# Weights on 128 partitions and a TensorE loop over all 32 tiles, in a decode attention kernel

## The chip, the cores and the metric

The kernel runs on one core of a Trainium2 chip. The metric is device time in microseconds (us) of one execution. Names used below: PE is TensorE (matmuls), DVE VectorE, ACT ScalarE, POOL GpSimd, SP SyncE, whose queue issues all DMA loads here. The page is the profiler's summary of one execution, and the span is the length of that execution in the profile.

## The reference

One decode step for a batch of 4. Four query rows attend to a cache of 8192 keys and values in 8 KV heads, and the result is gated by a small MLP branch. The part that costs time is the cache: 4 x 8 = 32 (batch, head) pairs, each with 4 MB of K and 4 MB of V.

```python
xn = layernorm(A_x)                               # 4 x 448
q  = xn @ wq                                      # wq 448 x 4096 -> 16 heads of 256
p  = softmax(q . k_cache * 256**-0.5)             # per (batch, kv head): 8192 keys, 2 query heads
s  = (p . v_cache) @ wo                           # wo 4096 x 448
xn2 = layernorm(xn)
g  = silu(xn + gelu(xn2 @ w3) @ w4)               # w3 448 x 1792, w4 1792 x 448 (w1, w2 drop out at S = 1)
out = A_x + s * g
```

## The kernel before

A "tile" is one (batch, KV head) pair. For tile h, PE transposes K in 16 groups (T), DVE and ACT copy the transposes out of PSUM, PE makes the scores (S), and softmax follows. PE multiplies with V one tile later (PV), in the last six slots of tile h + 1. K and V have two buffers each. SP issues the loads in this order (cut):

```python
sp.dma_start(wq_sb..., A_wq.rearrange("(p j) n -> p (j n)", j=4))   # 112 partitions, 32 KB each
sp.dma_start(w3_sb..., B_w3.rearrange("(p j) n -> p (j n)", j=4))   # 112 partitions, 14 KB each
sp.dma_start(w4_sb..., B_w4.rearrange("(p k) n -> p (k n)", k=14))  # 128 partitions, 12.25 KB each
load_k(0); load_k(1); <load wo>; load_v(0)
for h in range(2, NH):
    load_k(h)          # waits until tile h-2 is transposed
    load_v(h - 1)      # waits until PV of tile h-3 is done
load_v(NH - 1)         # in four pieces
```

448 = 4 x 112, so `wq` and `w3` lie on 112 partitions. On PE the first two tiles were straight code, because tile 0 has no tile before it, and a loop did the other 30:

```python
body(0, prev=False)
body(1, first=True)
with nc.Fori(0, (NH - 2) // 2, engines=[PE], ...):
    body(2); body(3)
<scores, softmax and PV of the last tile, output projection>
```

All other engines run straight code for all 32 tiles.

## Time and profile before

677.12 us was the median of the first three runs. The table holds the quantities that matter; the fences show where they are read.

| Quantity | Before |
|---|---|
| data moved, span of the profiled run | 279 MB, 675.8 us |
| DMA rate in most slices | 431 to 434 GB/s |
| PE busy | 80% |
| DMA rate in the first 25 us | 210 to 308 GB/s |
| instruction packets of PE (queue 8) | 14 |

From the page of the kernel before: the span, PE and the DMA rate in 40 equal slices, and the DMA queues.

```profile
span 675.8 us, 27268 instructions
...
PE   0675687898788789888787988887888888878987
...
GB/s 237 367 402 426 431 430 427 394 433 434 433 434 431 431 433 433 431 429 431 433 430 434 433 434 433 431 431 433 433 427 431 431 433 433 433 434 433 433 412 47
...
q1 hardware_dynamic: 14176, 279.00, 97.6%
q8 instruction: 14, 0.23, 0.1%
q14 instruction: 9, 0.07, 0.0%
```

The flat 431 to 434 of most slices is taken as the limit: 279 MB at 433 GB/s alone take 644 us. The exceptions are the first three slices, slice 8 and the end. `q8` and `q14` are instruction fetches.

The same kernel in windows. Columns: window, its length, busy time and number of instructions of each engine, the granted PE clock, the DMA share and GB/s.

```profile
0.00:5.00 5.00, 0.00 (x0) 0.00 (x0) 2.34 (x10) 1.49 (x2) 1.53 (x10) 1.00 0.81 210
5.00:10.00 5.00, 1.09 (x8) 0.97 (x8) 3.57 (x14) 1.49 (x2) 0.00 (x0) 1.00 0.84 216
10.00:15.00 5.00, 0.00 (x0) 0.00 (x0) 0.00 (x0) 0.00 (x0) 0.00 (x0) 1.00 1.14 308
15.00:20.00 5.00, 2.08 (x78) 2.11 (x79) 0.00 (x0) 0.00 (x0) 0.00 (x0) 1.00 0.86 212
20.00:25.00 5.00, 2.27 (x70) 2.21 (x68) 0.48 (x4) 0.00 (x0) 0.31 (x2) 1.00 0.98 305
25.00:30.00 5.00, 3.11 (x48) 2.81 (x47) 1.25 (x6) 0.25 (x1) 0.00 (x0) 1.00 1.07 456
...
120.00:125.00 5.00, 2.32 (x71) 2.20 (x68) 1.38 (x2) 0.00 (x0) 0.00 (x0) 0.74 0.78 331
```

Until 25 us the DMA engines are busy (share 0.81 to 1.14) and yet move 210 to 308 GB/s, half to 0.7 of what they move later (the first window also holds 2.1 us in which no weight packet has started). So they have work; their packets are slow. In the window at 120 us the share falls: there they had no work.

Why they had none is in the timelines of PE and of the SP queue, before. "[2.49 <-issue]" is idle time ahead of an instruction that waited for nothing the profile shows. In these lines `kn` is a K tile, `vb` a V tile, and `pst`, `psc` and `psv` are the PSUM results of T, S and PV.

```profile
102.17 0.62 PE L463 MATMUL psv<-pT,vb 128*128 128x32 bf16 x17 [2.49 <-issue]
109.49 0.33 PE L436 MATMUL psc<-qc,kT 128*128 128x2 bf16 x7 [1.15 <-issue]
116.84 0.39 PE L463 MATMUL psv<-pT,vb 128*128 128x32 bf16 x9 [2.33 <-issue]
123.75 0.48 PE L424 MATMUL pst<-ident_b,kn 128*128 128x128 bf16 x3 [2.68 <-issue]
```

```profile
102.82 0.33 SPq L174 DMA_DIRECT2D vb<-in_A_v_cache_dram  x1
124.26 0.33 SPq L161 DMA_DIRECT2D kn<-in_A_k_cache_dram  x1
```

PE stops inside groups of identical matmuls. In the trace's packet records a 16 KB packet of queue 8 belongs to each stop (99.8, 106.9, 114.5, 121.2 us): it starts with the stop, in the second case 1.4 us before it, and PE goes on 1.3 to 1.5 us after each of these packets has ended. This is the loop's first round, and its code is only now fetched. After one at 125.1 us there is no more such packet until the tail (669.7). So the loop, two tiles with 1,556 matmuls and weight loads (389 of each per tile, by the counts on the page), is fetched once. Because of the stops the K load at 124.26 us was issued late.

### The profile page before, as it was taken

Reading aid. Unit: us, or ns where it says so; the run is one execution under the profiler, and the core shown is the slowest. Engines: PE = TensorE matmul, PEld = TensorE weight load, DVE = VectorE, ACT = ScalarE, POOL = GpSimd, SP = SyncE. Lnnn points to the kernel's source line nnn. Section 1 sums busy time; section 2 is a strip of 40 time slices with the busy share of each in tenths; the row PEclk is TensorE's granted clock in tenths of the full one; section 3 lists DMA queues with packets and bytes.
Section 4 is the critical chain, followed back from the end, with each engine's and each line's share of the span. In section 5 each row is a group of like instructions: output and inputs, shape, how many; then the busy total and the mean of one; then the engine's idle time right before and its main releaser. Section 6 shows DMA issues by size and latency. Waiting matters only on the chain. (4 is left out here: it accounts for less than half of the span.)

```text
span 675.8 us, 27268 instructions
## 1 busy us (share of the span) xinstructions
PE 540.1 (80%) x12686; PEld 526.7 (78%) x12686; DVE 241.1 (36%) x550; ACT 250.1 (37%) x358; POOL 7.4 (1%) x42
## 2 busy tenths in 40 slices
PE   0675687898788789888787988887888888878987
PEld 0575687898788789888787988877888888878985
DVE  3143133343333334333333433433333433333432
ACT  1043143354333344343233443433344333334440
POOL 0000000000000000000000000000000000000000
PEclk9978688798878998788789987888997877889889
DMA  9999999999999999999999999999999999999991
GB/s 237 367 402 426 431 430 427 394 433 434 433 434 431 431 433 433 431 429 431 433 430 434 433 434 433 431 431 433 433 427 431 431 433 433 433 434 433 433 412 47
DMA packets 14199, 279.29 MB, mean 413 GB/s; under 512 B 1145, under 2 KB 5249, under 8 KB 5249
## 3 DMA queue, kind: packets, MB, share of 16 engines
q1 hardware_dynamic: 14176, 279.00, 97.6%
q8 instruction: 14, 0.23, 0.1%
q14 instruction: 9, 0.07, 0.0%
HBM read 278.99 MB, written 0.00 MB: 413 GB/s over the span
## 5 line engine op out<-in xcount | busy, mean ns | idle before, releaser
L424 PE MATMUL pst<-ident_b,kn 128*128 128x128 bf16 x4096 | 363.9, 241 | 87.7 <-PEq L385 81.2
L221 ACT ACTIVATE kT<-pst 128x1024 bf16<-128x1024 bf16 x224 | 227.1, 1024 | 363.3 <-PE pst L424 363.3
L424 PEld LDWEIGHTS pst<-ident_b,kn 128*128 128x128 bf16 x4096 | 279.8, 108 | 94.4 <-issue 93.1
L219 DVE COPY kT<-pst 128x1024 bf16<-128x1024 bf16 x288 | 199.1, 692 | 388.3 <-PE pst L424 388.3
L436 PE MATMUL psc<-qc,kT 128*128 128x2 bf16 x4096 | 181.6, 165 | 1.9 <-issue 1.9
L436 PEld LDWEIGHTS psc<-qc,kT 128*128 128x128 bf16 x4096 | 169.6, 101 | 3.0 <-issue 3.0
L463 PE MATMUL psv<-pT,vb 128*128 128x32 bf16 x3968 | 128.6, 177 | 20.7 <-PEq L385 12.5
L463 PEld LDWEIGHTS psv<-pT,vb 128*128 128x128 bf16 x3968 | 113.4, 96 | 18.5 <-issue 18.5
L241 ACT ACTIVATE pT<-psc,negb 128x64 bf16<-128x64 f32 x64 | 20.2, 331 | 19.0 <-DVE negb L338 19.0
L212 POOL COPY qc<-qT 128x4 bf16<-128x4 bf16 x32 | 5.9, 187 | 620.4 <-PE psc L436 600.5
L241 ACT ACTIVATION_READ_ACCUMULATOR pT<-psc,negb 128x1 f32 x64 | 12.6, 196 | 0.0
L450 PE MATMUL psm<-diag,ones_f 2*128 2x2 f32 x64 | 12.1, 256 | 0.0
L455 PE MATMUL psm<-rowsum,ones_f 128*128 128x2 f32 x64 | 11.8, 254 | 0.0
L399 PE MATMUL pst<-xnT,vb 112*128 112x4 bf16 x128 | 3.6, 166 | 8.4 <-PEq L385 8.4
L450 PEld LDWEIGHTS psm<-diag,ones_f 2*128 2x128 f32 x64 | 9.4, 182 | 1.0 <-issue 0.4
L399 PEld LDWEIGHTS pst<-xnT,vb 112*128 112x128 bf16 x128 | 3.5, 104 | 8.4 <-issue 8.4
L455 PEld LDWEIGHTS psm<-rowsum,ones_f 128*128 128x128 f32 x64 | 9.8, 192 | 0.4 <-issue 0.4
L350 DVE TENSOR_TENSOR OT<-psv,rz 128x2 bf16<-128x2 f32 x63 | 7.4, 162 | 7.4 <-PE psc L518 3.1
L446 PE MATMUL psm<-ident_f,rmax 128*2 128x128 f32 x32 | 9.4, 294 | 0.6 <-PEq L385 0.6
L326 DVE TENSOR_REDUCE rmax<-psc 128x2 f32<-128x128 f32 x32 | 9.0, 281 | 0.4 <-PE psc L436 0.4
L331 DVE TENSOR_REDUCE gmax<-psm 2x1 f32<-2x128 f32 x32 | 8.6, 269 | 0.6 <-PE psm L446 0.6
L392 PE MATMUL pst<-ident_b,xn_b 4*112 4x4 bf16 x8 | 1.1, 236 | 8.5 <-DVE xn_b L279 5.9
(59 smaller groups left out, 68.0 us busy)
## 6 DMA issues: line engine op xcount, KB each, us to landing
kn<-in_A_k_cache_dram SPq DMA_DIRECT2D x32, 4096.0 KB, 23.1
vb<-in_A_v_cache_dram SPq DMA_DIRECT2D x31, 4096.0 KB, 32.1
vb<-in_A_v_cache_dram SPq DMA_DIRECT2D x4, 1024.0 KB, 17.7
vb<-in_A_wq_dram SPq DMA_DIRECT2D x1, 3584.0 KB, 16.6
wo_sb<-in_A_wo_dram SPq DMA_DIRECT2D x1, 3584.0 KB, 54.3
vb<-in_B_w_dram SPq DMA_DIRECT2D x2, 1568.0 KB, 24.6
x_sb<-in_A_x_dram SPq DMA_DIRECT2D x1, 3.5 KB
out_dram<-out_b SPq DMA_DIRECT2D x1, 3.5 KB
```

The source lines that it names most:

```text
L219: engine.tensor_copy(dst, src).then_inc(S["v_ev"], 1)
L221: engine.activation(dst, src, ACT.Copy).then_inc(S["a_ev"], 1)
L241: ins = act.activation(pv_p[:, :, hh], sc[:, :, hh], ACT.Exp, bias=negb[:, s, hh:hh + 1], scale=SCALE, accum_out=rowsum[:, s, hh:hh + 1])
L326: v.tensor_reduce(rmax[:, :], psc[h % 2][:, 0:NCH * REP].rearrange("p (k h) -> p h k", h=REP), AX.X, ALU.max).then_inc(S["v_rmax"], 1)
L331: c(v.tensor_reduce(gmax[:, :], psm[0:REP, 0:P], AX.X, ALU.max))
L350: ins = v.tensor_tensor(OT[:, g, :, dh, b], src[:, dh * PVW:dh * PVW + REP], rz[:, :], ALU.mult)
L424: ins = pe.transpose(dst[:, t * P:(t + 1) * P], kn[:, h % 2, GC * j + kl, half * P:(half + 1) * P], ident_b[:, :])
L436: ins = pe.matmul(psc[h % 2][:, kk * REP:(kk + 1) * REP], kT[:, j % RING, t * P:(t + 1) * P], qc[:, h % 2, half, :], start=(half == 0), st ...
L446: pe.transpose(psm[0:REP, 0:P], rmax[:, :], ident_f[:, :]).then_inc(S["p_m1"], 1)
L450: pe.matmul(psm[:, P:P + REP], ones_f[0:REP, :], diag[:, :], start=True, stop=True).then_inc(S["p_m2"], 1)
L455: pe.matmul(psm[:, P + REP:P + 2 * REP], ones_f[:, :], rowsum[:, h % 2, :], start=True, stop=True).then_inc(S["p_m3"], 1)
L463: ins = pe.matmul(psv[:, dh * PVW:(dh + 1) * PVW], vb[:, h % 2, kk, dh * P:(dh + 1) * P], pT[:, h % 2, kk * REP:kk * REP + PVW], start=(kk ...
```

## The change

The intent: use all 128 partitions for the weights, and let one PE loop do all 32 tiles, with a dummy tile of zeros as the predecessor of tile 0. The core of the diff (cut):

```diff
-            sp.dma_start(wq_sb..., A_wq.rearrange("(p j) n -> p (j n)", j=DJ))
+            sp.dma_start(vflat[1][:, 0:DK * HDH],
+                         A_wq.rearrange("d (t n) -> (d t) n", t=NHF).rearrange("(p j) n -> p (j n)", j=DK))
 ...                                        # w3 the same; DK = 7, NHF = 2; w4 in two halves per partition
-                elif h == 1:
-                    sp.wait_ge(S["p_q"], 1)
-                    sp.wait_ge(S["p_pv"], h - 1)
+                    sp.wait_ge(S["p_pv"], h)
 ...
+            c(gp.memset(vflat[1][:, DK * HDH:NCH * DH], 0.0))      # what the dummy's matmuls read
+            c(gp.memset(qc[:, 1]..., 0.0)); c(gp.memset(kT[:, (NGR - LAG) % RING:RING, :]..., 0.0))
 ...
-                c(v.tensor_copy(dst_b[:, :], dst_f[:, :]))
+                <six small copies into a layout of 7 x 128>        # twice: two layernorms
 ...
-                v.tensor_copy(dst[0:DP], xT_ps[0:DP, k])
+                <four copies, multiplied with a mask of even and odd partitions>
 ...
-            body(0, prev=False)
-            body(1, first=True)
-            with nc.Fori(0, (NH - 2) // 2, ...):
-                body(2); body(3)
+            with nc.Fori(0, NH // 2, ...):
+                body(0); body(1)
```

448 x 2 = 7 x 128: each weight row is cut into two halves, the 896 half rows lie seven to a partition, and the mask keeps the halves apart in the product.

## The prediction

> **What bounds the kernel.** The DMA queue. The page moves 279 MB, most slices at 431 to 434 GB/s; 279.0 MB at 433 GB/s alone would take 644 of the 675.8 us. PE is busy 80%, but waits some 3 us for K at nearly every tile (waits view: 81 us on K transposes, 28 waits). By the timeline the end is the landing of the next-to-last V, its PV (654 to 660.5 us) and a fixed tail of 15 us: a DMA stream earlier by x moves the end by x.
>
> **Where DMA loses time** (packet records against a line of 433 GB/s):
> - start-up, 2.1 us;
> - weights, about 8.3 us by t = 27. `wq`, 112 packets of 32 KB, takes 1.99 us each; the same size takes 1.22 us in the K and V loads. `w3` (112 of 14 KB): 0.89 us; `w4`, on 128 partitions, 0.47 us for 12.5 KB. In 5 us windows the rate is 210 to 308 GB/s until 25 us, then 426 to 456. [...];
> - `wo`, 896 B packets, about 1.5 us, unchanged;
> - 1.5 us near 121 to 124 us: the queue ran dry, because the K load that waits for tile 3's transposes was issued only at 124.3. PE had gaps inside tiles 2 and 3 with no dependency (99.7, 108.3, 114.5, 121.1 us; 8.7 us in all), each at a 16 KB instruction packet. After 125 us, with the loop once round, there are none: the code of the two straight tiles and then of the loop is fetched cold.
>
> **What the change does.**
> 1. Three weights on 128 partitions. Per DMA engine, estimated from these packet times: `wq` 8 x 1.06 us, `w3` 8 x 0.47, `w4` 16 halves x 0.24: 16.2 us instead of 24. Gain 8.0 us, all on the stream.
> 2. The straight tiles go; the loop's cold round falls in tiles 0 and 1, while K1, `wo` and V0 are queued, so its stalls[...] are hidden and the dry queue disappears: 1.5 us. Instruction packets fall from 14 to about 8.
> 3. Added: 24 score, 128 PV and a few small matmuls in tile 0 (some 5 us of PE), memsets, five more small copies per layernorm (about 1.3 us each), eight masked copies for two. PE should reach tile 0 at about 27 us, K0 lands near 29.5: hidden. V1 waits for the dummy's PV, about 1 us after K2's issue, V0 still queued: hidden.
>
> Steady tiles and tail stay.
>
> **Prediction.** 677.1 - 8.0 - 1.5 + 0.2 for small things: **667.8 us**, range 665.8 to 670.5. Faster by over 2%: 0.04; within 2%: 0.95; slower by over 2%: 0.01.
>
> **What would show it.** Right: over 400 GB/s from 5 us on; K0 landing near 29.5 us instead of 38.5; no DMA dip between 100 and 130 us; undepended PE gaps only in tiles 0 and 1; tail still 15 us. Wrong: weight packets still slow[...]; PE late for K0; a new dry spot near 45 to 75 us, because cold stalls plus dummy work delay K2, V1 or K3.
>
> **What would make it wrong.** Step 1 if the slow start has another cause; step 2 if the cold round moves the dry spot instead of hiding it; a lower granted clock that makes PE the limit.

The 8.0 us rest on the packet times alone. The lengths under 3 are estimates. In the trace of the kernel before, 24 score matmuls took 0.74 us and the 128 of PV 4.1 us (from 654.12 us on, in six groups of 0.68 to 0.70), together the "some 5 us". The longer copies of a layernorm turned out to cost 1.1 to 1.2 us more (1.56 and 1.48 us in the changed kernel's first trace, beside 0.38 before).

## The result, and the profile after

The changed kernel took 670.49 us (median of 4, 669.10 to 671.38) beside 677.75 us before; ratio 0.9891, 95% interval 0.9865 to 0.9917. Two repeats gave 669.58 us, ratio 0.9886 (0.9864 to 0.9907), and 669.31 us, ratio 0.9863 (0.9840 to 0.9887). A ratio is the mean time of one kernel's runs over that of the other's of the same rounds, so it is not quite the ratio of the medians. The result lies inside the predicted range (665.8 to 670.5), in the first measurement by 0.01 us, which is luck, with two of its four runs above the upper edge; the medians of the repeats lie 0.9 and 1.2 us below that edge. The central value was 667.8.

The page of the changed kernel:

```profile
span 669.6 us, 27595 instructions
...
GB/s 353 439 397 437 431 433 427 433 435 431 429 433 431 438 427 431 435 431 431 432 427 437 435 431 427 433 435 435 427 431 433 431 433 435 427 433 433 433 374 5
...
q8 instruction: 9, 0.15, 0.1%
q14 instruction: 8, 0.07, 0.0%
```

Its windows, with the columns as above:

```profile
0.00:5.00 5.00, 0.00 (x0) 0.00 (x0) 2.75 (x8) 1.28 (x1) 4.47 (x11) 1.00 0.61 201
5.00:10.00 5.00, 0.32 (x7) 0.27 (x7) 4.25 (x18) 0.54 (x3) 1.70 (x3) 1.00 1.03 442
10.00:15.00 5.00, 1.92 (x69) 1.94 (x70) 3.45 (x17) 1.15 (x1) 0.00 (x0) 1.00 0.94 400
15.00:20.00 5.00, 4.09 (x105) 4.01 (x102) 1.06 (x5) 0.00 (x0) 0.19 (x1) 1.00 1.04 434
...
120.00:125.00 5.00, 5.00 (x162) 4.92 (x157) 2.06 (x3) 1.64 (x2) 0.00 (x0) 1.00 1.00 433
```

The first slow 25 us are gone (the first window again holds 2.1 us before the first weight packet), and so is the dip at 120 us. The K load that was issued at 124.26 us is now issued at 105.80:

```profile
105.80 0.33 SPq L169 DMA_DIRECT2D kn<-in_A_k_cache_dram  x1
```

The PE timeline of the changed kernel has its stops without a dependency in tiles 0 and 1 only; three of the five (the others last 0.5 and 0.6 us):

```profile
49.15 0.58 PE L499 MATMUL psv<-pT,vb 128*128 128x32 bf16 x17 [2.21 <-issue]
...
56.72 0.33 PE L473 MATMUL psc<-qc,kT 128*128 128x2 bf16 x7 [2.54 <-issue]
...
71.08 0.33 PE L461 MATMUL pst<-ident_b,kn 128*128 128x128 bf16 x3 [1.47 <-issue]
```

Each load of weights, K or V left 16 updates of its semaphore in the trace, taken here as one report from each of the 16 DMA engines. PE starts after the last: before, `wq`'s last report came at 17.8 us and its first matmul at 17.92, V30's at 654.0 and the first PV matmul at 654.12. So a load counts as landed with its last report. The next table is worked out from the reports and is used from here on: each cell is the first and the last report of one load, in us. "Weights only" is the first experiment below.

| Load | Before | Weights only | Changed |
|---|---|---|---|
| wq | 16.4 - 17.8 | 11.6 - 12.8 | 11.7 - 12.3 |
| K1 | 46.2 - 48.3 | 38.6 - 41.4 | 38.6 - 40.8 |
| V1 | 84.9 - 87.1 | 77.3 - 80.1 | 77.3 - 79.4 |
| K3 | 94.6 - 96.8 | 87.0 - 89.8 | 87.1 - 89.1 |
| V2 | 104.3 - 107.8 | 96.7 - 101.1 | 96.8 - 98.9 |
| K4 | 114.0 - 117.7 | 106.4 - 110.8 | 106.5 - 108.6 |
| V3 | 123.7 - 127.4 | 116.1 - 120.5 | 116.2 - 118.3 |
| K5 | 135.8 - 137.1 | 128.1 - 130.2 | 125.9 - 128.0 |
| K30 | 621.5 - 624.8 | 613.8 - 616.8 | 611.6 - 615.6 |
| V30 | 650.7 - 654.0 | 643.0 - 646.9 | 640.7 - 645.7 |

In first reports the stream is 10.0 us earlier at V30 (650.7 to 640.7). In last reports, for which PE waits, it is 8.3 us earlier (654.0 to 645.7). The first trace of the changed kernel is only 6.2 us shorter (675.8 to 669.6). The missing 2.1 us lie on PE. A part of 0.4 us comes ahead of PV: PE waited for V30 before, but in the first trace of the changed kernel it reached the PV of tile 30 without a wait, 0.5 us after V30 had landed. Its work on the last K tile, begun in a half-clock window (635.0 to 641.8 us by the clock records), was the later gate there. The first PV matmuls of tile 30, before and changed (first trace):

```profile
654.12 0.68 PE L463 MATMUL psv<-pT,vb 128*128 128x32 bf16 x21 [0.37 <-PEq L385]
```

```profile
646.22 0.68 PE L499 MATMUL psv<-pT,vb 128*128 128x32 bf16 x21
```

The larger part, 1.7 us, lies in the 24 matmuls of the output projection. Timelines: before, changed (first trace), changed (second trace).

```profile
663.29 4.70 PE L504 MATMUL pst<-wo_sb,OT 128*4 128x448 bf16 x24
```

```profile
655.39 6.39 PE L537 MATMUL pst<-wo_sb,OT 128*4 128x448 bf16 x24
```

```profile
654.69 4.70 PE L537 MATMUL pst<-wo_sb,OT 128*4 128x448 bf16 x24
```

The same instructions took 1.7 us longer in the first trace. Its windows show why (the last three numbers of a line are the granted clock, the DMA share and GB/s):

```profile
654.00:656.00 2.00, 1.96 (x9) 0.84 (x10) 0.65 (x3) 0.30 (x2) 0.00 (x0) 0.87 0.03 12
656.00:658.00 2.00, 2.00 (x7) 0.72 (x6) 0.00 (x0) 0.40 (x4) 0.00 (x0) 0.50 0.00 0
658.00:660.00 2.00, 2.00 (x10) 0.81 (x9) 0.00 (x0) 0.00 (x0) 0.00 (x0) 0.78 0.00 0
```

The clock was 0.50 for 3.4 us, from 655.5 to 658.9 us by the clock records. In the clock records of this trace and of the kernel before, every stretch is at 1.00 or 0.50 and, but for the one cut off by the end, one or several times 3.41 us long. In the second trace the clock stayed at 1.00 there and the span was 667.2 us. The 14 timed runs of the changed kernel fall into two groups with nothing between: ten at 669.0 to 669.8 us and four at 671.1 to 671.4. The traced executions fit: the one of 671.38 us had the half clock on the projection, those of 668.99 and 669.26 us had not.

### The profile page after: what moved, and what is told of

It is laid out like the page before. It is cut to its first block, busy times and chain, and to the rows that moved or that the text cites. A ratio compares the mean times of both kernels' runs of the same rounds, so it can differ in the third digit from the quotient of the medians.

```text
span 669.6 us, 27595 instructions
## 1 busy us (share of the span) xinstructions
PE 546.1 (82%) x12826; PEld 531.9 (79%) x12826; DVE 246.7 (37%) x572; ACT 250.3 (37%) x362; POOL 12.1 (2%) x45
## 5 line engine op out<-in xcount | busy, mean ns | idle before, releaser
L499 PE MATMUL psv<-pT,vb 128*128 128x32 bf16 x4096 | 132.6, 177 | 11.2 <-PEq L415 8.4
L499 PEld LDWEIGHTS psv<-pT,vb 128*128 128x128 bf16 x4096 | 116.9, 96 | 12.3 <-issue 12.3
L421 PE MATMUL pst<-ident_b,xn_b 4*128 4x4 bf16 x14 | 0.6, 161 | 12.8 <-DVE xn_b L295 8.1
L421 PEld LDWEIGHTS pst<-ident_b,xn_b 4*128 4x128 bf16 x14 | 0.5, 100 | 12.8 <-issue 8.1
L537 PE MATMUL pst<-wo_sb,OT 128*4 128x448 bf16 x32 | 8.2, 416 | 0.4 <-PEq L415 0.4
```

The costliest lines, as they stand in the source:

```text
L499: ins = pe.matmul(psv[:, dh * PVW:(dh + 1) * PVW], vb[:, h % 2, kk, dh * P:(dh + 1) * P], pT[:, h % 2, kk * REP:kk * REP + PVW], start=(kk ...
L537: ins = pe.matmul(o_ps[0:Bn, 0:D], OT[:, g, hh, dh, :], wo_sb[:, k, :], start=(k == 0), stop=(k == NKC - 1))
```

## The experiments

Theory after the first look: (a) 112 partitions made the weight packets slow; (b) the stream is as late as its slowest DMA engine, and what delays that engine is instruction packets, not the queue that ran dry; (c) the rest of the shortfall is the half clock in the tail. Rivals stand in the expectations. The DMA engines of single packets are not named in the trace, so (b) is tested by adding and removing packets, and by asking which of the 16 reports of a load move.

**Weights only.** The new weights and their preparation, with the straight tiles, waits and loop of before (the diff is cut to the loop).

```diff
-            with nc.Fori(0, NH // 2, ...): body(0); body(1)
+            body(0, prev=False); body(1, first=True)
+            with nc.Fori(0, (NH - 2) // 2, ...): body(2); body(3)
```

> Weights on 128 partitions, the two straight tiles kept, no dummy. Main theory: the dry spot of the kernel before (1.5 us on the mean engine) cost the slowest engine nothing, because that engine never ran dry; so the loop change is worth 0 to 1 us and this kernel comes at 669.5 to 671.5 us, within 1 us of the changed kernel; the spread between first and last landing of one tile falls from about 3.5 us to 1.3 to 2 us at the dry spot. Rival (the prediction's sum): the loop change is worth 1.5 us and this kernel comes 1.5 us above the changed kernel, about 672.

Measured: 671.45 us, ratio to before 0.9906 (0.9884 to 0.9927), beside 669.58 us for the changed kernel in the same rounds. So the loop half is worth 1.9 us by medians and 1.6 by means; at V30's last report it is 1.2 us (646.9 to 645.7), or 1.5 against the repeat's 645.4. In amount the rival, which was the prediction's sum, is the better one. The dry spot is there again, in its windows:

```profile
110.00:115.00 5.00, 3.52 (x112) 3.40 (x110) 1.38 (x2) 1.02 (x1) 0.00 (x0) 1.00 1.02 436
115.00:120.00 5.00, 3.80 (x71) 3.80 (x71) 1.61 (x4) 0.51 (x1) 0.00 (x0) 0.54 0.83 318
120.00:125.00 5.00, 5.00 (x97) 4.95 (x96) 2.74 (x7) 2.84 (x5) 0.19 (x1) 0.78 0.99 426
```

But the table above shows that it is not where the last reports lost time. Across the dry spot they come 9.7 us apart (K4 110.8, V3 120.5, K5 130.2), the normal step for 4 MB, while the first reports step by 12.0 (116.1 to 128.1). By these reports the slowest engine had work all the time; the others waited for it, and the spread shrank from 4.4 to 2.1 us. The last reports lost their time one load earlier, K3 to V2: 11.3 us here, 11.0 before, 9.8 in the changed kernel. Two 16 KB packets of PE's code were fetched in that stretch (93.0 and 100.7 us; before, 99.8 and 106.9), and none in the changed kernel. The 16 reports show that one engine lost it: from K3 to V2, in the three traces with the old loop (before, this one, and the run with cuts below), the last report slips by 1.3 to 1.5 us against the first and the other fifteen by at most 0.1; in the traces with the new loop none does. That it is a packet of PE's code that delays this engine is inferred from the times; the first of the two is the likelier, because the second ends (101.7 us here, 108.0 before) after V2's last report.

**The changed kernel again.**

> The changed kernel once more, for a tighter ratio and a second trace. Main theory: the DMA stream's end is set by the slowest of the 16 DMA engines; it is earlier by 8.3 us and not by 9.3, and the tail of 22 us after the landing of the next-to-last V is lengthened by 1.7 us in those executions in which a half-clock window of 3.4 us falls on the output projection. Expect 669.0 to 671.5 us, in two clusters about 1.7 us apart; landing of the last engine of the next-to-last V again at 645 to 646.5 us. Rival: the shortfall is noise of the first four runs, and the median is 668.

Measured: 669.58 us, ratio 0.9886 (0.9864 to 0.9907); runs at 669.0 to 669.7 and at 671.2; V30's last report at 645.4. As the main theory said; the rival's 668 was not met. The third measurement belongs to the last experiment of this section.

**Partitions or position.** The kernel before, with `w4` first, and the last V's four quarters, in the middle of the steady stream, cut by partitions.

```diff
+            <w4 load>                       # first, then wq, w3
-            <V31 quarter i: 128 partitions, one DMA>
+            cut = (112, 64, 96, 128)[i]
+            <V31 quarter i: partitions 0:cut and cut:128, two DMAs>
```

> The kernel before with the weights' order changed (w4, on 128 partitions, goes first, then wq and w3 on 112) and the last V's four quarters (8 KB per partition, in the middle of an undisturbed stream) cut by partitions: first quarter 112 + 16, second 64 + 64, third 96 + 32, fourth 128 whole. Main theory (the partitions that a load covers set its packet times): w4's 12.5 KB packets take 0.47 us although they are the first, wq's 32 KB packets again about 2.0 us; 8 KB packets take 0.31 us whole, about 0.5 us in the 112 part[...]. Rival (early reads of HBM are slow, whatever the shape): w4's packets take 0.75 us, wq's 1.2 to 1.6, and all 8 KB packets 0.31 us.

Measured (one look, one run, 682.6 us, correct): `w4`'s packets had a median of 0.47 us, from 2.1 us on, as first load; `wq`'s, now in second place, averaged 1.97 us (1.99 before). The 8 KB packets of V31 took 0.58 us on average for the first 128 and 0.31 before; only the last ones, of the whole quarter, went back to 0.31. The four kinds of cut overlap in time and can't be told apart. The windows of this run over V31:

```profile
650.00:655.00 5.00, 5.00 (x101) 4.91 (x99) 2.46 (x7) 3.52 (x7) 0.00 (x0) 0.91 0.90 213
655.00:660.00 5.00, 3.13 (x78) 3.10 (x76) 0.72 (x3) 1.09 (x2) 0.00 (x0) 0.77 1.02 210
660.00:665.00 5.00, 5.00 (x163) 5.00 (x159) 2.27 (x5) 1.02 (x1) 0.00 (x0) 0.89 1.01 197
665.00:670.00 5.00, 4.38 (x27) 1.99 (x24) 0.94 (x4) 0.70 (x4) 0.00 (x0) 1.00 1.01 211
```

The kernel before moved 393 and 423 GB/s in the windows at 650 and 655 us, with the same bytes from the same tensor. So the partitions decide, not the place in time: the rival falls. (Each cut also makes two loads of one; that cutting as such is slow was not tested apart, but `wq`, uncut, was slow in both places.) Why the packets of a load on fewer partitions are slow (1.99 against 1.22 us, and 197 to 213 GB/s for the mixture of cuts) is not shown.

**More VectorE code.** Eight memsets of one column at the end of each tile.

```diff
                 f_ot(h - 1)
+                for i in range(8):
+                    v.memset(pad[:, h * 8 + i:h * 8 + i + 1], 0.0)
```

> The changed kernel with 8 tiny VectorE memsets (one element on four partitions) at the end of each tile: 256 instructions more, 0.5 us per tile on an engine that is busy 37%. Main theory: VectorE's straight code is fetched in 8 KB packets of 128 instructions, all on one DMA engine, and each delays that engine by about 1 us: two more packets by 645 us, spread between first and last landing of the next-to-last V from 5.0 to 7.0 us, kernel 1.5 to 2.5 us slower than the changed one. Rival (the spread has another cause, or VectorE's fetches don't count): same time within 0.5 us, spread still 5.

Measured: 672.27 us, ratio 0.9913 (0.9893 to 0.9934), 2.7 us above the changed kernel in the same rounds by medians and 2.2 by means. V30 reported from 640.8 to 647.6: the first engine unmoved, the last 2.2 us later than the repeat's 645.4, spread 6.8 us. The 8 KB packets of the kind that comes about once in 130 VectorE instructions (133 on average in the trace of the kernel before, 128 in the changed one's) went from four to six by 645 us. The rival falls; of the 2.7 us, 2.2 are this delay. The rest need not come from the packets: in the traced execution of 672.9 us the 24 projection matmuls took 6.39 us, as in the slow group of the changed kernel. Of V30's 16 reports only the last moved clearly: the one before it came 2.4 us after the first, beside 2.6 in the repeat. So the added packets delay one engine.

**Less VectorE code.** The two products that scale a tile's PV result merged into one (the last tile keeps two).

```diff
+                if h < NH - 1:
+                    v.tensor_tensor(OT[:, g, :, :, b].rearrange("p hh dh -> p dh hh"),
+                                    psv[:, 0:NHALF * PVW].rearrange("p (dh w) -> p dh w", w=PVW)[:, :, 0:REP],
+                                    rz[:, :].unsqueeze(1).to_broadcast([P, NHALF, REP]), ALU.mult)
+                    return
                 for dh in range(NHALF): ...
```

> The changed kernel with the two small VectorE products per tile merged into one: 31 instructions fewer. Main theory: the fourth 8 KB packet of VectorE's code moves from 616 us to after 645 us, too late to delay the next-to-last V: spread 4.0 instead of 5.0 us, its last landing at 644.7 instead of 645.7 us, kernel about 1 us faster than the changed one. Rival: no change beyond 0.3 us.

Measured: 668.36 us, ratio 0.9861 (0.9839 to 0.9882), 1.2 us under the changed kernel. The fourth packet moved from 616 to 654 us, V30's last report to 644.7, spread 3.9. The 16 reports agree: from K30 to V30 the last report slips by 1.0 us against the first in all three traces of the changed kernel, and by less than 0.1 in the four traces with the merged product. A repeat on another chip took 668.46 us:

> The merged-product kernel again, as the one that the two runs before are compared with on the same chip: 668.2 to 670 us in both theories, spread of the next-to-last V's landing 3.9 us.

As expected there too (V30's last report at 644.5, spread 3.5; ratio 0.9849, 0.9823 to 0.9874).

**PV in the last slot.** On the merged kernel.

```diff
-    PV_SLOTS = tuple(range(10, 16))
+    PV_SLOTS = (15,)
```

> The merged-product kernel (e3) with the 128 PV matmuls of the tile before all in the last slot instead of spread over six. Theory (the end is the landing of the next-to-last V, what PE still has to do after it, and the tail): after that landing PE has 128 PV matmuls (about 4 us) instead of six slots of transposes, scores and PV (6.5 us), so 2 to 2.5 us faster than e3, with the same DMA stream. Rival (the end hangs on the last V's landing): no change.

Measured: 669.17 us, 0.7 above the merged kernel in the same rounds, ratio 0.9862 (0.9837 to 0.9886). Both named outcomes missed. The PE timeline tells why ("PEq" is PE's own sequencer, here waiting for the K load):

```profile
634.94 0.91 PE L467 MATMUL pst<-ident_b,kn 128*128 128x128 bf16 x8 [2.63 <-PEq L421]
...
647.37 3.37 PE L505 MATMUL psv<-pT,vb 128*128 128x32 bf16 x128
650.59 0.74 PE L479 MATMUL psc<-qc,kT 128*128 128x2 bf16 x24
...
652.15 1.65 PE L543 MATMUL pst<-wo_sb,OT 128*4 128x448 bf16 x4
```

From the landing of the last K at about 635 us PE worked without a stop on the last tile's transposes and scores and reached PV at 647.4, almost 3 us after V30 had landed (644.5). So V30 was not the only gate: PE's own work since the last K's landing ends at nearly the same time, as in the first trace of the changed kernel. The move did gain something: the output projection began at 652.15 us, beside 652.83 in the trace of the merged kernel on the same chip. But a half-clock window (652.2 to 655.6 us) fell on it: its first four matmuls took 1.65 instead of 0.92 us. So this execution, which is the median one, hides a gain of 0.7 us ahead of the projection; how many of the other four runs met such a window is not known. The statement of the prediction that the end is V30's landing plus a fixed tail is too narrow. It did no harm to the sum, because K31 and V30 move together.

**No gaps in the tail.** Five matmuls of 512 columns into a free PSUM buffer, in the two waits ahead of the output projection, once on the merged kernel, once on the changed one.

```diff
+            warm(3)
             f_rmaxT(h)
 ...
             f_o(0)
+            warm(2)
             f_bc(h)
```

> The merged-product kernel (e3) with five filler matmuls of 512 columns in the two waits of the tail, so that TensorE has no gap there. Main theory: the half-clock window that fell on the output projection in the first trace of the changed kernel comes after a stretch with gaps; with the gaps filled the 24 projection matmuls take 4.7 us in every execution, and the slower cluster of times goes: median 668.0 or a little under, all runs within 1 us. Rival (the window's place is chance and has nothing to do with the gaps): times in two clusters as before, median within 0.3 us of e3's.

> The changed kernel with the five filler matmuls in the two waits of the tail. Ten timed runs of the changed kernel so far: six at 669.0 to 669.8 us, four at 671.2 to 671.4. Theory: the upper cluster is a half-clock window on the output projection, brought on by the gaps ahead of it; with the gaps filled no run is in the upper cluster (by chance alone that has odds of about 1 in 12 in five runs), the 24 projection matmuls take 4.7 us, median 669.2 to 669.7. Rival: the windows fall where they fall, one or two runs at 671.

> The changed kernel again on the same chip, for comparison: one to three of its runs in the cluster near 671.2 us, the others at 669.0 to 669.8, by both theories.

Measured: on the merged kernel 668.77 us (all four runs within 0.4; 668.46 without the filler), on the changed one 670.20 us (669.76 to 670.35; 669.31 without). The theory had a basis in the clock records: of the stretches at 0.50, 30 of 33 in the trace before and 32 of 34 in the first of the changed kernel began 1.1 to 4.5 us after the start of a PE gap of over 1.4 us. But the one at 655.5 us is among the exceptions: it came after 19 us in which PE had no gap over 0.63 us. No run with filler was in a slow group, but none without it was either on these two chips, against what both theories expected of the last run, so the test is inconclusive. The filler itself cost 0.3 and 0.9 us; both expected medians were missed by more than 0.4 us. What sets off the half clock in the tail, and whether the chip matters, stays open.

## Why the prediction was right or wrong

- **Bound by DMA: right.** The steady slices stayed at 427 to 438 GB/s and the whole gain lies in the stream.
- **Weights, 8.0 us: right in cause, 7.5 to 7.7 in size.** K1's last report moved from 48.3 to 40.8 and V1's from 87.1 to 79.4. The packet times were as estimated (`w3` 0.47, the `w4` halves 0.24, `wq`, now in packets of 28 KB, a median of 1.06 us), but the first `wq` packets were slower (mean 1.16). K0 landed at 30.7 us and not near 29.5: 7.8 us earlier than before. That partitions and not early reads made the packets slow is shown by the experiment with cuts; by what mechanism is not.
- **The dry queue, 1.5 us: the amount came, by luck; the reason was wrong.** By the prediction's packet records the average over 16 engines did lose 1.5 us there, but a load has landed with its slowest engine, and by the reports that one was never dry. What moved the last reports (by 7.7 us at K3 and 9.1 at K5, thus 1.4 from the loop) happened between K3 and V2, where the old code had PE's instruction packets on the queue and one engine slipped by 1.3 to 1.5 us. The step that failed is the reading of a mean rate as if it were the landing time.
- **Hidden additions: right for time on PE, DVE and POOL, wrong as code.** Tile 0 began at 30.8 us, just after K0's landing at 30.7. But VectorE's added code moved the fourth 8 KB packet of its code from 663 us, where it was harmless, to 616 us (the longer head alone, in "weights only", to 637; the rest came with the new loop and its dummy tile). The advance of last reports fell from 9.2 us at K30 to 8.3 at V30. The merge and the padding experiments show this delay in both directions.
- **"Steady tiles and tail stay": the tail term failed in part.** In the first trace PE was 0.4 us late at PV, and a half-clock window cost 1.7 us in the output projection; in the two repeats there was none in the trace, and their spans were 8.6 and 8.3 us below before.

Sum: 7.7 + 1.4 - 0.9 = 8.2 us (the advance at V30 is 8.3), and in four runs of fourteen about 1.9 less. The prediction had 9.3. By times alone this is not excluded (the third measurement has 678.63 and 669.31 us, a gain of 9.3); that the stream gained less is read from the traces.

The merged kernel, at 668.4 us, has the lowest median of all versions run. Its ratio's interval overlaps that of the changed kernel; that it is faster rests on V30's reports, too.

## What to carry to other kernels

Here a load had landed when its slowest DMA engine had (V30 before: first report 650.7 us, last 654.0, PV from 654.12): look at the spread between first and last report before you cost a dip in the mean rate. On the saturated queue here, instruction fetches were traffic too (about 1 us on one engine per 8 KB packet, which is 0.3 us long by its own record), so straight code, even on an engine off the critical path, delayed the data (256 VectorE instructions more: 2.2 us at V30), and a loop that went round early hid its fetches (1.4 us at K5). Lay big loads on all 128 partitions: here 112 cost more than the missing eighth (1.99 us per 32 KB packet against 1.22).
